# V of later batches loaded in single pieces at five places, and k's transposes over DRAM scratch issued a score step sooner, in a fused attention and SwiGLU kernel

## The chip, the cores and the metric

The kernel runs on one core of a Trainium2 chip. The metric is the device time of one execution in microseconds (us). The time before is the median of three runs.

## What is computed

Attention over 8 batches of 8 heads, 576 tokens and 64 channels, with a causal mask and a bias from a running sum; its output, as 4608 tokens of 512 channels, goes through a gated feed-forward block.

```python
scores = scale * np.matmul(q, k.transpose(0, 1, 3, 2))
cum = np.cumsum(np.maximum(s, 0.0), axis=-1)
bias = -(cum[:, :, :, None] - cum[:, :, None, :])
scores = np.where(causal, -1000000000.0, scores + np.minimum(bias, 0.0))
attn = softmax(scores)
attn_out = np.matmul(attn, v)
x = attn_out.transpose(0, 2, 1, 3).reshape(B * S, H * D)
out = (silu(x @ w_gate) * (x @ w_val)) @ w_out
```

## The kernel before

Each engine has its own queue and runs it in the order in which the program writes it; the program writes that order by hand. SP computes nothing: it issues DMAs, one after the other, and stops at one whose wait is not over.

**Attention.** The 64 heads are worked through in half-batches of 4 heads: half-batch `h`, score step `step` (0 to 3, one head), and in each step four pieces `ci` (0 to 3) of the score matrix. `score_piece` (line 352) lets PE multiply k and q (L373) into a PSUM bank and ACT write the exponentials to `pt` (L383). One step later PE multiplies `pt` with V (L410), and DVE divides by the row sums (L426, L427) into `ot`, which holds a pair of heads. There are 8 banks; a bank is free again when ACT or DVE has read it.

**The way of k and q.** Two half-batches ahead, SP loads k and q as float32 (`load_qk`, L145, tiles `rawk` and `rawq`), ACT casts them to bfloat16 (`cast_one`, L258, `ck` and `cq`), SP writes them to DRAM scratch (`scratch`, L274, `ks` and `qs`), SP reads them back transposed (`transposes`, L284, `pk` and `pq`, one buffer each), and DVE copies them to the operands of the score matmuls (`split`, L288). The splits wait in a list `later`, out of which `do_later` issues one for every two or four pieces of feed-forward work.

**The way of V.** Five pieces for each batch, 128 tokens of 8 heads in each (the last 64), loaded by SP (`load_v`, L162) into `rawv`, which has one buffer, and cast to `vt` by ACT (L171) in steps 1 to 3 of the batch's preceding odd half-batch. For batch 2 POOL casts (L173).

**The way of the output.** From batch 2 on, POOL stores each pair of heads to DRAM (`x_out`, L444, `xs`), and SP reads it back transposed (`x_in`, L451) into `XT`, two steps after the pair's last scores, in one or two parts. `XT` holds three token tiles of 512 tokens in a ring.

**Feed-forward.** There are nine token tiles `tt`. For each, PE multiplies XT with the weights of gate and value (L643), four contraction slices for each product, of which slice `c` is the pair of heads `c` of the batch; ACT takes a tanh (L664), DVE multiplies (`pp` L666, `ht` L677); then PE multiplies with the output weights (L700 for tiles 0 and 1, L749 for the rest). The main loop interleaves this with attention: after every piece of feed-forward work, attention goes on up to a set position. Tile 2 begins 3.6 steps after the scores of batch 2 are done.

**The places.** `side(h, step, ci)` is called behind every score piece and says what is issued there. For half-batches from 7 on: at step 0, piece 1 the raw loads of half-batch `h + 3`; at step 2, piece 0 both scratch writes of `h + 2`; at step 3, piece 0 the pending splits and both transposes of `h + 2`; in even half-batches V pieces 0 and 1 at step 2, piece 1 and pieces 2 to 4 at step 3, piece 1. For half-batch 6 (`six`, issued in `h = 4`) the places of scratch and transposes are step 3, piece 0 and step 3, piece 3. The XT transposes come behind the last piece of steps 1 and 3.

Of the kernel before, what the change touches and what calls it, by code (L numbers as in the profile page):

```python
# [19 lines left out]
def kernel(  # L20
# [11 lines left out]
    nc = tc.nc  # L32
# [10 lines left out]
    NR = HB // 2  # L43
    J = 9
# [37 lines left out]
    KS = {i: dram.tile([NR * S, 128], BF16, name=f"ks{i}") for i in range(NPE, NHB)}  # L82
# [3 lines left out]
    QS = {i: dram.tile([NR * S, 128], BF16, name=f"qs{i}") for i in range(NPE, NHB)}  # L86
# [27 lines left out]
    with tc.manual_schedule():  # L114
# [37 lines left out]
        def load_qk(hb):  # L152
            load_one(hb, "k")
            load_one(hb, "q")

        def load_v(b, cs, eng=nc.sync):
            if 0 in cs:
                loaded["v", b] = raw.tile([128, NCH, H, D], FP32, tag="rawv", bufs=1, name="rawv")
            t = loaded["v", b]
            for c in cs:  # L160
                n = 128 if c < 4 else TAIL
                eng.dma_start(  # L162
                    t[0:n, c, :, :],
                    v[b, :, c * 128 : c * 128 + n, :].rearrange("h p d -> p h d"),
                )

        def cast_v(b, c, eng):
            n = 128 if c < 4 else TAIL
            dst, src_t = VT[b % 2][0:n, c, :, 0:D], loaded["v", b][0:n, c, :, :]
            if eng is nc.scalar:  # L170
                nc.scalar.copy(dst, src_t)  # L171
            else:
                eng.tensor_copy(dst, src_t)  # L173
# [9 lines left out]
        def aug(hb, engs, hhs=range(HB)):  # L183
            for hh in hhs:
                r, e = divmod(hh, 2)
                r0 = 64 * (1 - r)
                bh = hb * HB + hh
                engs[hh].dma_start(  # L188
                    KQ[hb % 2][r][r0 : r0 + 4, :, e * S : (e + 1) * S],
                    HL[bh : bh + 1, :, :, :],  # L190
                )
# [61 lines left out]
        def cast_one(hb, name, eng):  # L253
            cts[name, hb] = cp.tile([128, J, NR, D], BF16, tag="c" + name, bufs=2, name="c" + name)
            dst = cts[name, hb].rearrange("x j r d -> x r j d")
            src_t = loaded[name, hb]
            if eng is nc.scalar:
                nc.scalar.copy(dst, src_t)  # L258
            else:
                eng.tensor_copy(dst, src_t)  # L260
# [8 lines left out]
            else:  # L269
                eng.tensor_copy(dst, src_t)  # L270

        def scratch(hb):
            for name, SC in (("k", KS), ("q", QS)):
                nc.sync.dma_start(  # L274
                    SC[hb].rearrange("(x j) c -> x (j c)", j=J),
                    cts[name, hb].rearrange("x j r d -> x (j r d)"),
                )

        prs = {}

        def transposes(hb):
            for name, SC in (("k", KS), ("q", QS)):
                prs[name, hb] = cp.tile([128, NR * S], BF16, tag="p" + name, bufs=1, name="p" + name)
                nc.sync.dma_start_transpose(prs[name, hb], SC[hb])  # L284

        def split(hb, name, r):
            kq = SRC[name][1]
# [181 lines left out]
        later = []  # L469

        def do_later(n):
            while n > 0 and later:
                f, *args = later.pop(0)
                f(*args)
                n -= 1
# [5 lines left out]
        def side(h, step, ci):  # L481
            bh = HB * h + step
            for c in V1_AT.get((bh, ci), ()):
                cast_v(1, c, nc.gpsimd)
            if bh == H + 4 and ci == 3:
                load_v(2, range(5))
            if h == 4 and (step, ci) in ((0, 1), (2, 1)):
                load_qk(6 + step // 2)
            if h >= 5 and h + 3 < NHB and (step, ci) == (0, 1):
                load_qk(h + 3)  # L490
            hb = h + 1
            if NPE <= hb < NHB:
                late = hb == NPE
                if late and (step, ci) == (0, 1):
                    scratch(hb)
                if late and (step, ci) == (0, 3):
                    transposes(hb)
                if (step, ci) == (0, 1):
                    aug(hb, GP4)
                first = 1 if hb < NPE + 3 else 0  # L500
                if step in (first, first + 1) and ci == (3 if late else 1):
                    for r in range(NR):
                        later.append((split, hb, "kq"[step - first], r))
            hb = h + 2
            if hb == NPE and step == 3 and ci % 2 == 1:
                cast_one(hb, "kq"[ci // 2], nc.gpsimd)
            if NPE < hb < NHB:
                six = hb == NPE + 1
                if (step, ci) == ((2, 0) if six else (0, 2)):
                    cast_one(hb, "k", nc.scalar)  # L510
                if (step, ci) == ((2, 2) if six else (1, 2)):
                    cast_one(hb, "q", nc.scalar)
                if (step, ci) == ((3, 0) if six else (2, 0)):
                    scratch(hb)
                if (step, ci) == (3, 3 if six else 0):
                    do_later(NR * 2)
                    transposes(hb)
            if ci != 1:
                return
            bn = h // 2 + 1  # L520
            if 3 <= bn < B:
                if h % 2 == 0:
                    if step == 2:
                        load_v(bn, (0, 1))
                    if step == 3:
                        load_v(bn, (2, 3, 4))

        V2_AT = {(1, 0): 0, (1, 1): 1, (1, 2): 2, (1, 3): 3, (2, 0): 4}
        V_AT = {(1, 0): 0, (2, 0): 1, (2, 2): 2, (3, 0): 3, (3, 2): 4}

        def side_v(h, step, ci):
            bn = h // 2 + 1
            if h == 4 and (step, ci) in V2_AT:
                cast_v(2, V2_AT[step, ci], nc.gpsimd)
            if 3 <= bn < B and h % 2 == 1 and (step, ci) in V_AT:
# [25 lines left out]
        def attn_items():  # L561
            for kk in range(H, BH + 2):
                h, step = divmod(kk, HB)
                if kk < BH:
                    if step == 0:
                        do_later(NR * 2)
                    if step == 1 and 3 < h + 1 < NPE:
                        cast_one(h + 1, "k", nc.gpsimd)
                        cast_one(h + 1, "q", nc.gpsimd)
                    if step == 2 and 3 < h + 1 < NPE:  # L570
                        aug(h + 1, GP4)
                    for ci in range(4):
                        score_piece(kk, ci)
                        side(h, step, ci)
                        side_v(h, step, ci)
                        yield kk + 0.1 + ci / 8
                        if (step, ci) in PREP_AT.get(h, ()):
                            prep_one(
                                h + 1, PREP_AT[h][step, ci],
                                (nc.scalar, nc.vector)[ci // 2] if h == 2 else None,  # L580
                            )
                            yield kk + 0.1 + ci / 8
# [327 lines left out]
        def pick(side):  # L910
            b = PICK[side]
            for lo in range(2):
                for c0, c1 in ((0, 512), (512, S)):
                    nc.tensor.matmul(
                        banks[:, b + c0 // 512, 0 : c1 - c0], sel[:, lo, :],
                        HL[:, lo, 1, c0:c1], start=(lo == 0), stop=(lo == 1),
                        skip_group_check=True,
                    )

        def picked_row(side):  # L920
            b = PICK[side]
            src_t = banks.rearrange("p b n -> p (b n)")[up, b * 512 : b * 512 + S]
            dst = KQ[0][0][up, side, 0:S]
            if side == 1:
                nc.scalar.activation(
                    dst, src_t, AF.Identity, bias=r_m[up, 0:1], scale=r_k[up, 0:1]
                )
            else:
                nc.vector.tensor_scalar(
                    dst, src_t, r_q[up, :], r_k[up, :], ALU.mult, ALU.add  # L930
                )
            give(b)
            give(b + 1)
# [102 lines left out]
        at = attn_items()  # L1036
# [84 lines left out]
```

## Time and profile before

| what | us |
|---|---|
| median of 3 runs | 374.26 (373.94 to 375.38) |
| the profiled execution | 373.92 |
| its span, first to last instruction | 372.0 |
| its granted TensorE clock | 0.998 of full speed |

The chain of work that ended last, by engine, and the two kinds of DMA queue (the hardware queue is SP's, the software queue POOL's):

```profile
PE 83%; DVE 10%; DMA 2%; ACT 2%; issue 2%; POOL 1%; DVEq 0%; ACTq 0%
...
q1 hardware_dynamic: 84964, 41.46, 46.9%
q0 software_dynamic: 12128, 22.21, 22.7%
```

The second and third line give packets, megabytes and the share of the 16 DMA engines' time. In a row of the order of time, the numbers are the start and the duration in us, then the engine (SPq: SP's queue), the line, what is written from what, how often, and in brackets the idle time before it and what ended it. For SP's DMAs the duration is that of the issue; when one has landed is seen in the semaphores, which count to sixteen for each DMA. In the waits, the three numbers are us in total, times, and the longest. A row of DMA packets counts those below a size cumulatively.

### The profile page before, as it was taken

How to read it: one execution, taken by the hardware profiler on the slowest of the kernel's cores; microseconds unless marked ns; L12 is line 12 of the kernel's file. 1: busy time of each engine (PE TensorE's matmuls, PEld its weight loads, DVE VectorE, ACT ScalarE, POOL GpSimd, SP SyncE). 2: the span in 40 equal slices, each digit the busy share in tenths (PEclk: the TensorE clock that was granted, in tenths of full speed). 3: DMA queues.
4: the chain of work that ended last, by engine and by line, in shares of the span. 5: the costliest groups of instructions: out<-in, count | busy, mean ns of one | idle time of the engine just before them, and what ended most of it. 6: DMA issues, size and time to landing. Idle time of an engine off the chain costs nothing.

```text
span 372.0 us, 8786 instructions
## 1 busy us (share of the span) xinstructions
PE 363.2 (98%) x3288; PEld 230.3 (62%) x3288; DVE 291.1 (78%) x585; ACT 239.9 (65%) x470; POOL 212.4 (57%) x325
## 2 busy tenths in 40 slices
PE   7899999999999999999999999999999999999996
PEld 6684556655555557855685558655865585476465
DVE  8978776377985899589967897699868867975984
ACT  8877776778886967688757875786565523323321
POOL 8983556955266547594749464955675516315320
PEclk9999999999999999999999999999999999999999
DMA  7999999799879996996789484994142113002003
GB/s 238 220 254 259 215 272 257 239 299 227 252 172 307 199 268 181 162 285 217 214 179 263 160 185 157 265 210 114 40 121 62 35 30 118 0 3 86 28 0 113
DMA packets 97133, 64.21 MB, mean 173 GB/s; under 512 B 77228, under 2 KB 82724, under 8 KB 97092
## 3 DMA queue, kind: packets, MB, share of 16 engines
q1 hardware_dynamic: 84964, 41.46, 46.9%
q0 software_dynamic: 12128, 22.21, 22.7%
q8 instruction: 25, 0.41, 0.5%
q14 instruction: 16, 0.13, 0.1%
HBM read 37.90 MB, written 19.86 MB: 155 GB/s over the span
## 4 chain that ended last, share of the span: by engine, by line
PE 83%; DVE 10%; DMA 2%; ACT 2%; issue 2%; POOL 1%; DVEq 0%; ACTq 0%
PE banks L643 43%; PE banks L749 17%; PE banks L373 9%; PE banks L410 7%; PE banks L700 5%; DVE kq L330 3%; DMA pk<-ks 2%; DVE pp L666 2%; DVE ht L677 1%; DVE kq L288 1%; ACT th L664 1%; POOL vt L173 1%; ACT pt L383 1%; PE banks L459 1%; PE banks L301 0%
## 5 line engine op out<-in xcount | busy, mean ns | idle before, releaser
L383 ACT ACTIVATE pt<-banks 128x512 bf16<-128x512 f32 (+1 forms) x256 | 120.4, 511 | 29.8 <-PE banks L373 17.1
L643 PE MATMUL banks<-XT,wg 128*128 128x512 bf16 x432 | 111.4, 379 | 0.4 <-DVE pp L666 0.3
L643 PE MATMUL banks<-XT,wv 128*128 128x512 bf16 x432 | 110.9, 379 | 0.1
L664 ACT ACTIVATE th<-banks 128x512 bf16<-128x512 f32 x108 | 64.7, 599 | 56.3 <-PE banks L643 51.4
L666 DVE SCALAR_TENSOR_TENSOR pp<-th,banks 128x512 bf16<-128x512 bf16 x108 | 73.7, 682 | 18.3 <-ACT th L664 18.0
L677 DVE SCALAR_TENSOR_TENSOR ht<-pp,banks 128x512 bf16<-128x512 bf16 x108 | 74.1, 687 | 10.3
L373 PE MATMUL banks<-kq 128*128 128x128 bf16 (+4 forms) x576 | 76.4, 240 | 0.8 <-DVE kq L330 0.3
L686 POOL TENSOR_TENSOR ht<-ht 128x512 bf16<-128x512 bf16 x35 | 40.4, 1154 | 53.3 <-DVE su L684 53.2
L373 PEld LDWEIGHTS <-kq 128*128 128x128 bf16 x576 | 46.1, 98 | 30.7 <-issue 2.4
L643 PEld LDWEIGHTS <-wv 128*128 128x128 bf16 x432 | 38.4, 98 | 36.2 <-issue 0.2
L643 PEld LDWEIGHTS <-wg 128*128 128x128 bf16 x432 | 38.4, 98 | 34.1 <-issue 0.7
L410 PEld LDWEIGHTS <-pt 128*128 128x128 bf16 x960 | 41.8, 98 | 17.7 <-issue 0.7
L388 POOL TENSOR_SCALAR_AFFINE_SELECT pt<-pt 128x512 bf16<-128x512 bf16 x56 | 36.6, 653 | 25.9 <-ACT pt L383 21.7
L410 PE MATMUL banks<-vt,pt 128*128 128x65 bf16 x960 | 46.8, 194 | 0.5 <-DVE ot L427 0.4
L444 POOL DMA_DIRECT2D xs<-ot x24 | 21.7, 904 | 30.4 <-DVE ot L427 28.0
L749 PEld LDWEIGHTS <-ht 128*128 128x128 bf16 x336 | 31.2, 98 | 4.3
L427 DVE TENSOR_TENSOR ot<-banks,rc 128x320 bf16<-128x320 f32 x64 | 31.5, 492 | 2.2
L188 POOL DMA_DIRECT2D kq<-HL x48 | 29.2, 610 | 0.0
L700 PE MATMUL banks<-wo,ht 128*128 128x512 bf16 x96 | 25.8, 379 | 0.0
L749 PEld LDWEIGHTS <-su 128*128 128x128 bf16 x252 | 23.6, 98 | 3.3
L814 POOL TENSOR_TENSOR ysb<-ysb 128x512 f32<-128x512 f32 x12 | 15.2, 1269 | 15.3 <-DVE ysb L808 15.3
L749 PE MATMUL banks<-WS,ht 128*128 128x256 bf16 x168 | 22.9, 273 | 0.0
(101 smaller groups left out, 377.2 us busy)
## 6 DMA issues: line engine op xcount, KB each, us to landing
out_dram<-ysb POOLq DMA_DIRECT2D x32, 256.0 KB, 4.0
rawv<-in_v_dram SPq DMA_DIRECT2D x28, 256.0 KB
rawk<-in_k_dram SPq DMA_DIRECT2D x12, 576.0 KB
rawq<-in_q_dram SPq DMA_DIRECT2D x12, 576.0 KB
xs<-ot POOLq DMA_DIRECT2D x24, 160.0 KB, 3.7
ks<-ck SPq DMA_DIRECT2D x11, 288.0 KB
qs<-cq SPq DMA_DIRECT2D x11, 288.0 KB
rawk<-in_k_dram POOLq DMA_DIRECT2D x3, 576.0 KB, 6.0
```

Source lines behind the costliest of these rows:

```text
L373: nc.tensor.matmul(sc[:, o : o + w], T[:, 1, e * S + 128 * tj : e * S + 128 * (tj + 1)], T[:, 0, e * S + lo : e * S + hi], start=not maske ...
L383: nc.scalar.activation(pt[:, c0 : c0 + n], sc, AF.Exp, scale=0.125)
L388: nc.gpsimd.affine_select(pt[:, 1088:1600], pt[:, 1088:1600], pattern=[[0, 4], [1, 128]], compare_op=ALU.is_ge, fill=zreg, base=0, channel ...
L410: nc.tensor.matmul(av[:, bi * (D + 1) : (bi + 1) * (D + 1)], pt[:, c0 : c0 + 128], VT[b % 2][:, tj, h, :], start=(tj == 0), stop=(tj == bi),)
L427: nc.vector.tensor_mul(ot[:, :, e * D : (e + 1) * D], av3[:, :, 0:D], rc[:, :, None].to_broadcast([128, NCH, D]),)
L643: nc.tensor.matmul(view(bs, TT), w[:, c, f0 : f0 + 128], xt[:, c, :], start=(c == 0), stop=(c == 3),)
L664: nc.scalar.activation(th, pg, AF.Tanh, scale=0.5)
L666: nc.vector.scalar_tensor_tensor(pp, in0=th, scalar=1.0, in1=pg, op0=ALU.add, op1=ALU.mult)
L677: nc.vector.scalar_tensor_tensor(hp[:, 2 * k2 : 2 * k2 + 2, :].rearrange("p a n -> p (a n)"), in0=pp, scalar=0.5, in1=pv, op0=ALU.mult, op ...
L686: (nc.vector if ft == NFT - 1 else nc.gpsimd).tensor_sub(hp[:, 1:3, :], hp[:, 1:4:2, :], hp[:, 0:3:2, :])
L700: nc.tensor.matmul(view(pys[ts_], DM), hps[ft // 2][:, 2 * (ft % 2) + half, c0 : c0 + 128], WO[j][:, ft % WKO, :], start=(ft == 0), stop=( ...
L749: nc.tensor.matmul(ps, lhs(p), rhs(p), start=(first and p == 0), stop=(last and p == NP - 1), skip_group_check=True,)
```

## The change

V from batch 3 on is no longer issued in groups of two and three pieces but one piece at each of five places: from batch 4 on at step 0 piece 3, step 1 pieces 0 and 2, step 2 piece 1 and step 3 piece 1 of the even half-batch; for batch 3, pieces 0 and 1 at step 2 pieces 1 and 3 of half-batch 4, and pieces 2 to 4 at step 0 pieces 1 and 3 and step 1 piece 1 of half-batch 5. The scratch write of k goes to step 1 piece 1 (q's stays), the transposes of k to step 2 piece 2 (q's stays at step 3 piece 0); for half-batch 6 to step 2 piece 1 and step 3 piece 1 (q's stay). Before the transposes of a name, only the pending splits up to the last of that name are issued.

```diff
-        def scratch(hb):
-            for name, SC in (("k", KS), ("q", QS)):
+        SCR = {"k": KS, "q": QS}
+
+        def scratch(hb, names="kq"):
+            for name in names:
                 nc.sync.dma_start(
-                    SC[hb].rearrange("(x j) c -> x (j c)", j=J),
+                    SCR[name][hb].rearrange("(x j) c -> x (j c)", j=J),
                     cts[name, hb].rearrange("x j r d -> x (j r d)"),
                 )
...
-        def transposes(hb):
-            for name, SC in (("k", KS), ("q", QS)):
+        def transposes(hb, names="kq"):
+            for name in names:
+                while any(args[1] == name for _, *args in later):
+                    do_later(1)
                 prs[name, hb] = cp.tile([128, NR * S], BF16, tag="p" + name, bufs=1, name="p" + name)
-                nc.sync.dma_start_transpose(prs[name, hb], SC[hb])
+                nc.sync.dma_start_transpose(prs[name, hb], SCR[name][hb])
...
+                if (step, ci) == ((2, 1) if six else (1, 1)):
+                    scratch(hb, "k")
                 if (step, ci) == ((3, 0) if six else (2, 0)):
-                    scratch(hb)
-                if (step, ci) == (3, 3 if six else 0):
-                    do_later(NR * 2)
-                    transposes(hb)
-            if ci != 1:
-                return
+                    scratch(hb, "q")
+                if (step, ci) == ((3, 1) if six else (2, 2)):
+                    transposes(hb, "k")
+                if (step, ci) == ((3, 3) if six else (3, 0)):
+                    transposes(hb, "q")
             bn = h // 2 + 1
             if 3 <= bn < B:
-                if h % 2 == 0:
-                    if step == 2:
-                        load_v(bn, (0, 1))
-                    if step == 3:
-                        load_v(bn, (2, 3, 4))
-
+                at = VLOAD_AT if bn > 3 else V3LOAD_AT
+                if (h % 2, step, ci) in at:
+                    load_v(bn, (at[h % 2, step, ci],))
+
+        VLOAD_AT = {(0, 0, 3): 0, (0, 1, 0): 1, (0, 1, 2): 2, (0, 2, 1): 3, (0, 3, 1): 4}
+        V3LOAD_AT = {(0, 2, 1): 0, (0, 2, 3): 1, (1, 0, 1): 2, (1, 0, 3): 3, (1, 1, 1): 4}
```

In a key of the two tables the first number is `h % 2`, the second the step, the third the piece; the value is the piece of V.

## Prediction

> **What bounds the kernel now.** I read the engine shares and the slices of the page first, then the waits (all, and SP's own), then PE, ACT and SP in order of time from 70 to 140 us, then the DMA packets of short stretches.
>
> ```profile
> span 372.0 us, 8786 instructions
> PE 363.2 (98%) x3288; PEld 230.3 (62%) x3288; DVE 291.1 (78%) x585; ACT 239.9 (65%) x470; POOL 212.4 (57%) x325
> ...
> DMA  7999999799879996996789484994142113002003
> ```
>
> PE sets the end. Its rows run at one pace (four 512-column matmuls take 0.86 us wherever the chain shows them after 35 us) at a granted clock of 0.998, so PE can only lose time by standing idle. It is idle 372.0 - 363.2 = 8.8 us. I listed the gaps: all but two (and a few below 0.1 us) lie before 35 us, which the change doesn't touch. These are the two, and what DVE waited for:
>
> ```profile
> 83.34 0.38 PE L373 MATMUL banks<-kq 128*128 128x128 bf16 x4 [0.26 <-DVE kq L288]
> 131.44 0.47 PE L410 MATMUL banks<-vt,pt 128*128 128x65 bf16 x10 [0.40 <-DVE ot L427]
> ...
> DVE kq L288 <- DMA pk<-ks: 1.7, 2, 1.0
> ```
>
> So nothing that the change can do for PE is worth more than 0.26 + 0.40 = 0.66 us, 0.18% of 374.26. What it can cost is open, since the DMA slices mostly read 6 to 9 until about 205 us: whatever SP issues sooner pushes back what it issues later. The place where that matters is the start of token tile 2, at 116.41 us:
>
> ```profile
> 107.81 0.57 SPq L145 DMA_DIRECT2D rawk<-in_k_dram  x1
> 108.44 0.46 SPq L145 DMA_DIRECT2D rawq<-in_q_dram  x1
> 108.94 2.45 SPq L451 DMA_TRANSPOSE XT<-xs  x2
> 111.50 0.53 SPq L274 DMA_DIRECT2D ks<-ck  x1
> 112.12 0.38 SPq L274 DMA_DIRECT2D qs<-cq  x1
> 112.55 1.81 SPq L162 DMA_DIRECT2D rawv<-in_v_dram  x2
> 118.37 2.59 SPq L284 DMA_TRANSPOSE pk<-ks  x1
> ...
> 116.41 1.02 PE L643 MATMUL banks<-XT,wg 128*128 128x512 bf16 x4
> ```
>
> The transpose at 108.94 brings heads 22 and 23 of batch 2 into XT. They are the last of the four contraction slices of tile 2, so the fourth matmul of that row needs them, at 116.41 + 3 x 0.215 = 117.05 us. In the trace's semaphore record the first of the two transposes (the part that tile 2 reads) gets its sixteenth completion at 116.31, 7.4 us after its issue. The margin is 0.74 us. The same difference for tiles 3 to 6 is 5.0, 5.4, 4.1 and 4.7 us.
>
> **The change part by part.** PE's, ACT's and POOL's instructions stay the same and in the same order; no bank is taken or given elsewhere. What moves is SP's queue, and in DVE's queue at most a split copy by a place or two.
>
> *Splits forced early.* The k transposes now first issue the pending k splits. They run (L288) at 92.67 and 94.97, 106.99 and 108.81, 125.62 and 129.93, each at or before the new place (step 2, piece 2, for instance 94.97 and 130.18). So nothing or one copy moves: 0.45 us on DVE at most, hidden behind DVE's other waits; 0 on PE.
>
> *K scratch and transposes sooner.* For half-batch 6 the k scratch moves from 80.48 to just behind its cast (the ACT cast at 74.36 takes 1.15, so 75.5), ahead of V pieces. Its transposes should land about 88 instead of 92.6, and those of half-batch 8 one or two us before 125.6. That ends DVE's two waits of 1.7 us together. Gain on PE: between 0 and 0.66; I take 0.40, the gap at 131.44, since it follows the wait at 125.62. The gap at 83.34 belongs to half-batch 5, which isn't moved.
>
> *V of batch 3, pieces 2 to 4 later.* They move from behind the q scratch of half-batch 6 (83.85) to behind the raw loads of half-batch 8. Before, SP issues those at 93.91, 4.1 us after the q transposes (89.80). The q transposes now wait only for q's scratch (issued about 80.5, landing about 87), so the raw loads start near 91.1 and, with the 5.7 us that they took to land (93.91 to 99.58 in the semaphore record), end near 96.8. A V piece more: near 98.2. Its cast wants it at 95.45:
>
> ```profile
> 95.45 0.64 ACT L171 CAST vt<-rawv 128x512 bf16<-128x512 f32 x1
> ...
> 97.34 0.62 ACT L171 CAST vt<-rawv 128x512 bf16<-128x512 f32 x1
> ...
> 99.67 0.61 ACT L171 CAST vt<-rawv 64x512 bf16<-64x512 f32 x1
> ```
>
> ACT waits some 2.7 us (0.5 if SP gets there 2 us sooner, 4 if q's scratch lands at 88.25 as before). Behind that cast stand exponentials and tanh (95.95, 96.37, 96.87), and DVE's `pp` waits for the tanh. PE goes on while PSUM banks are free. From 95.25 to 98.44 PE begins five banks in 3.2 us and, every fourth us or so, one for V; about 1.8 a us. A bank is held some 1.6 us (tanh 0.60, `pp` 0.68 and the wait between), so 3 of 8 are held, and 5 last 2.8 us, about as long as ACT's wait. PE loses little here, 0.3 us (0 to 2, as DVE is busy 6.6 of 7 us from 94 to 101 and can't catch up). If PE is late here it is late at 117 too, so this is inside the next term, not on top of it.
>
> *V of batch 4, three pieces ahead of XT.* This decides. Before, between the raw loads of half-batch 9 (107.81, 108.44) and the XT transposes (108.94) SP issues nothing. After the change stand there, in SP's program order, V pieces 0 and 1, the k scratch of half-batch 8, and V piece 2. What does one cost? A V piece is 128 x 8 = 1024 rows of 256 B, a scratch 128 rows of 2304 B. Two stretches with a full queue:
>
> ```profile
> DMA packets 2277, 1.25 MB, mean 313 GB/s; under 512 B 2065, under 2 KB 2065, under 8 KB 2277
> ...
> DMA packets 2925, 0.80 MB, mean 201 GB/s; under 512 B 2879, under 2 KB 2879, under 8 KB 2924
> ```
>
> The first is 80 to 84 us (beside stores of POOL), the second 86 to 90. So 1024 short rows take 4 x 1024 / 2065 = 1.98 us or 4 x 1024 / 2879 = 1.42 us. In 76 to 80 us the same view has 455 packets above 2 KB and 241 below 512 B: (4 - 241 x 1.4/1000) / 455 = 8 ns each, so a scratch is 1.0 us. Three pieces and one scratch: 5.3 us (1.42) to 6.9 us (1.98). I take 5.3, as the semaphore record has V pieces 1.3 to 1.4 us apart just after (120.44, 121.74).
>
> *SP sooner.* Against this, the raw loads of half-batch 9 may be issued sooner. They follow the XT transposes of the pair before, whose store lands at 103.38; with 2.5 us for those two, 105.9 is the earliest, 1.9 us before 107.81. In between lies SP's longest wait for a scratch, which the change means to hide:
>
> ```profile
> SPq L284 <- DMA ks<-ck: 20.7, 7, 4.0
> ```
>
> It ends at 102.6. But q's scratch of half-batch 7 is now issued behind V pieces and XT transposes, and its transposes stand ahead of the XT ones, so part of the wait is only handed from k to q. Between 0 and 1.9 I take 1.2.
>
> The sum: 116.31 + 5.3 - 1.2 = 120.4 for the landing, against 117.05: PE idle 3.4 us. Less the 0.40 above: +3.0 us. All later XT parts have 4 to 5 us of margin, gain 3 more from PE's delay, and are moved less, since SP waits there for the store (up to 9.2 us) and the V pieces are through by then: 0. The profiled run took 373.92 (span 372.0, 1.92 around it), 0.34 below the median of 374.26; added to the median, 377.3.
>
> The Trainium skill's page "DMA: Bandwidth & Descriptors" (section "Queues, rings and completion order") says that each DMA engine takes a queue's descriptors in ring order; this trace agrees (the sixteenth completions of SP's transfers from 107.81 to 118.37 come in the order of issue). The same page's fit for one DMA (section "Anatomy of one DMA"), 2.0 us + bytes / 436e3, speaks against my price, though it is given for GpSimd's path: with the fixed part overlapped, a 256 KB piece would move in 0.60 us, three in 1.8, and with the scratch at 0.68 XT would land at 117.6, which makes the kernel 0.1 us slower, an estimate. The rows decide, and they have a piece at 1.42.
>
> **The rivals.**
> *A, absorbed.* The pieces cost less than in the rows or SP is the full 1.9 us sooner: with pieces at 1.0 us (two of the batch 3 ones land 1.03 apart, 89.05 and 90.08), 116.31 + 4.0 - 1.9 = 118.4, so 1.3 idle, less 0.4: 375.2. For it: pieces do land 1.0 apart at times. Against: POOL's stores of tile 1 share the engines just then.
> *B, not slower.* The transposes land in time, because SP's 4.0 us wait at 98.6 falls away and the DMA engines' idle time at 101 to 104 (share 0.21) is filled, so that everything issued up to XT is done sooner. It decides if XT's part lands by 117.05. Price: the 0.40 to 0.66 of the gaps: 373.6 to 373.9. Against: the store at 103.38 holds SP whatever is in front, so at most 1.9 of 5.3 can come back.
> *C, both waits in full.* The V casts hold ACT for 4 us with pieces 3 and 4 late too, SP is not sooner, and the pieces cost 1.98: XT at 116.31 + 6.9 = 123.2, 6.2 idle, less 0.4: 380.0. The q scratch waiting behind V speaks for it; the short rows at 1.42 against.
> *D, no effect.* The new places could coincide with when SP gets there anyway; SP runs behind its program in 80 to 125 us, so order is all that counts, and the order does change. I see little for this apart from A and B.
>
> **How the numbers follow.** A measurement of this kernel tells about 0.5%, 1.9 us, from no change. Forecast (+1.9 to +5): 0.62. C: 0.08. A and what else stays within 1.9 us: 0.20. B: 0.10, of which 0.03 beyond 0.5%, from a gain that I don't see. Faster 0.03, same 0.27, slower 0.70. The forecast's own range is 376.2 to 379.2; the one for 8 in 10 takes in A and the better part of B: 373.9 to 379.3.
>
> **What would show it.** Right: a new PE gap of 2 to 5 us at the fourth matmul of tile 2 (about 117), ended by the XT transposes; ACT waiting for rawv near 95 to 98; DVE no longer waiting for pk; SP rows with rawv ahead of XT. After 125 us both kernels run in parallel, shifted by a constant. Wrong: XT landing before 117 with the V pieces ahead of it (then the price of a piece was off), the gap ended by ACT or DVE instead (then the casts decide), or PE losing time at tiles 3 to 6 (then the stores, slowed by V, are what is late).

## The result

| | before | after |
|---|---|---|
| median of 22 runs, us | 374.04 (373.23 to 378.62) | 379.38 (375.51 to 381.75) |
| ratio of the times | | 1.0111, 95% interval 1.0091 to 1.0130 |
| span of the profiled execution, us | 372.0 | 378.0 |

The change makes the kernel slower by 1.1%, some 4.2 us; the medians are 5.3 us apart and the two profiled executions 6.0. A ratio here is of fast executions alone, without those more than 1.5% above the quickest of the same kernel, while a median is of all. The page of the changed kernel (its lines stand four to five further down in the code):

```profile
span 378.0 us, 8753 instructions
PE 363.5 (96%) x3248; PEld 231.5 (61%) x3288; DVE 291.6 (77%) x585; ACT 240.0 (64%) x470; POOL 212.4 (56%) x325
...
PE 82%; DVE 8%; DMA 4%; ACT 2%; issue 2%; POOL 1%; SPq 1%; DVEq 0%; ACTq 0%
```

PE is as busy as before, 363.5 us against 363.2, and the span is longer: most of the time went into idle PE. (Forty matmul records are missing here, 3248 of 3288; each leaves a false gap of 52 or 53 ns, some 2.1 us together.) In the chain the DMAs' share is 4% where it was 2%. These are PE's rows around the two places, with the idle time and what ended it in brackets:

```profile
99.58 0.19 PE L377 MATMUL banks<-kq 128*128 128x64 bf16 x1 [0.79 <-ACT pt L387]
100.79 1.02 PE L648 MATMUL banks<-XT,wv 128*128 128x512 bf16 x4 [1.02 <-DVE pp L671]
...
118.51 0.81 PE L648 MATMUL banks<-XT,wg 128*128 128x512 bf16 x3
121.92 0.38 PE L648 MATMUL banks<-XT,wg 128*128 128x512 bf16 x1 [2.60 <-DMA XT<-xs]
...
122.63 1.67 PE L648 MATMUL banks<-XT,wv 128*128 128x512 bf16 x4
124.09 1.91 PE L648 MATMUL banks<-XT,wg 128*128 128x512 bf16 x4
```

The first two gaps begin with ACT. Its cast of V piece 2 of batch 3, which stood at 95.45 before, waits:

```profile
98.79 0.62 ACT L171 CAST vt<-rawv 128x512 bf16<-128x512 f32 x1 [3.24 <-DMA rawv<-in_v_dram]
```

The third is the fourth matmul of token tile 2: XT isn't there. And behind it four matmuls take 1.67 and 1.91 us in place of 1.03, though PE waits for nothing. The windows of 2 us show why (busy us and instructions of PE, PE's weight loads, DVE, ACT and POOL; then the granted clock, the DMA share and GB/s):

```profile
120.00:122.00 2.00, 0.08 (x1) 0.08 (x1) 0.00 (x0) 0.00 (x0) 0.44 (x1) 1.00 0.69 161
122.00:124.00 2.00, 2.00 (x18) 1.02 (x18) 0.94 (x3) 1.08 (x2) 0.45 (x1) 0.72 0.99 376
124.00:126.00 2.00, 2.00 (x6) 0.76 (x5) 1.49 (x3) 0.00 (x0) 2.00 (x5) 0.50 1.26 264
```

The granted clock is 0.50 from 122.87 to 126.28 us. SP's rows (the number is the start and the duration of the issue) show how XT came to be late:

```profile
109.35 0.57 SPq L145 DMA_DIRECT2D rawk<-in_k_dram  x1
109.97 0.49 SPq L145 DMA_DIRECT2D rawq<-in_q_dram  x1
110.56 1.16 SPq L162 DMA_DIRECT2D rawv<-in_v_dram  x2
111.81 3.52 SPq L276 DMA_DIRECT2D ks<-ck  x1
115.38 0.43 SPq L162 DMA_DIRECT2D rawv<-in_v_dram  x1
115.91 3.57 SPq L455 DMA_TRANSPOSE XT<-xs  x2
```

Between the raw loads and the XT transposes stand three V pieces and a scratch, and XT is issued at 115.91 instead of 108.94. By the semaphore record its part for tile 2 lands at 121.88 instead of 116.31. SP wasn't waiting for the store of that pair of heads: POOL's store landed at 111.34, 4.6 us before XT was issued.

The same exponential of both kernels, found by its number on ACT, says where the 6.0 us arise:

| exponential, before at | after at | later by | what lies between |
|---|---|---|---|
| 92.97 | 92.97 | 0.0 | |
| 101.6 | 103.7 | 2.1 | V cast, 0.79 + 1.02 of PE's idle time |
| 118.0 | 122.9 | 4.9 | XT at tile 2 |
| 123.5 | 130.0 | 6.55 | clock at half rate, 1.7 |
| 133.2 | 139.2 | 6.0 | the gap at 131 is gone, which gives 0.56 |
| 293.45 (last) | 299.44 | 6.0 | nothing in the last 160 us of attention |

### The profile page after: what moved, and what is told of

Read it like the earlier page. It is cut to its first block, busy times and chain, and to the rows that moved or that the text cites. A ratio compares the mean times of both kernels' runs of the same rounds, so it can differ in the third digit from the quotient of the medians.

```text
span 378.0 us, 8753 instructions
## 1 busy us (share of the span) xinstructions
PE 363.5 (96%) x3248; PEld 231.5 (61%) x3288; DVE 291.6 (77%) x585; ACT 240.0 (64%) x470; POOL 212.4 (56%) x325
## 4 chain that ended last, share of the span: by engine, by line
PE 82%; DVE 8%; DMA 4%; ACT 2%; issue 2%; POOL 1%; SPq 1%; DVEq 0%; ACTq 0%
PE banks L648 43%; PE banks L754 17%; PE banks L377 9%; PE banks L414 7%; PE banks L705 4%; DVE kq L334 2%; DMA rawv<-in_v_dram 2%; DMA XT<-xs 2%; DVE pp L671 2%; DVE ht L682 1%; DMA kq<-HL 1%; ACT pt L387 1%; POOL vt L173 1%; ACT th L669 1%; PE banks L463 1%
## 5 line engine op out<-in xcount | busy, mean ns | idle before, releaser
L705 PE MATMUL banks<-wo,ht 128*128 128x512 bf16 x90 | 24.8, 379 | 0.3
L397 POOL TENSOR_SCALAR_AFFINE_SELECT pt<-pt 128x64 bf16<-128x64 bf16 x56 | 14.9, 266 | 17.4 <-ACT pt L387 17.2
```

Of the source, the lines that this page charges most:

```text
L705: nc.tensor.matmul(view(pys[ts_], DM), hps[ft // 2][:, 2 * (ft % 2) + half, c0 : c0 + 128], WO[j][:, ft % WKO, :], start=(ft == 0), stop=( ...
```

## The experiments

The theory: V of batch 3 behind the raw loads stops ACT, and V of batch 4 ahead of XT stops PE. The rivals: the new order of k's scratch and transposes costs the time; a late store decides; single pieces cost as such. Times are medians; ratios are to the kernel before on the same chip. Executions of one kernel differ by some us, often because of the first 60 us, where no version differs. So the profiles are compared by one stretch: from the exponential at 63.51 us to the last one, which takes 229.94 us in the kernel before. Landings in this table, and times of SP that are compared between versions, are given less what the execution had lost by the exponential at 63.51. The stretch and the landing are of one execution of each version.

| version | median us | ratio (95%) | stretch against before | XT lands |
|---|---|---|---|---|
| before | 374.0 to 375.1 | 1 | 0 | 116.3 |
| the change | 379.4 | 1.0111 (1.0091 to 1.0130) | +6.0 | 121.9 |
| k's moves alone | 375.0 | 1.0017 (0.9988 to 1.0046) | +1.0 | 115.9 |
| V alone | 379.5 | 1.0111 (1.0057 to 1.0166) | +1.7 | 119.3 |
| V of batch 4 back | 375.6 | 1.0049 (1.0017 to 1.0081) | +1.7 | 119.3 |
| V of batch 3 back | 378.8 | 1.0063 (1.0023 to 1.0102) | +4.6 | 120.6 |
| the same again | 377.5 | 1.0039 (1.0004 to 1.0074) | +1.4 | 119.0 |
| the same, PE kept busy | 378.0 | 1.0103 (1.0058 to 1.0148) | +2.6 | 120.2 |
| V of batches 3 and 4 back | 375.5 | 1.0007 (0.9972 to 1.0041) | -0.6 | 116.7 |
| one piece behind XT | 378.1 | 1.0072 (1.0038 to 1.0107) | +1.8 | 119.3 |
| the change, PE kept busy | 379.4 | 1.0098 (1.0061 to 1.0134) | +7.0 | 123.5 |
| all V behind XT | 374.8 | 0.9994 (0.9961 to 1.0026) | -0.6 | 115.6 |

**One half of the change at a time.** First k's scratch and transposes alone:

```diff
                 at = VLOAD_AT if bn > 3 else V3LOAD_AT
-                if (h % 2, step, ci) in at:
+                if True:
+                    if (h % 2, ci) == (0, 1) and step in (2, 3):
+                        load_v(bn, (0, 1) if step == 2 else (2, 3, 4))
+                elif (h % 2, step, ci) in at:
                     load_v(bn, (at[h % 2, step, ci],))
```

> Only the k scratch and the k transposes are moved; V stays in its groups of two and three. Theory (the V pieces cost the time): one scratch of about 1 us stands ahead of the XT transposes of heads 22 and 23, against 0.74 us of margin and a sooner SP, so PE waits 0 to 0.3 us at tile 2, ACT never waits for rawv, DVE's waits for pk go: 373.3 to 374.3 us, ratio 0.998 to 1.001. Rival (the new order of scratch and transposes costs the time): PE waits 2 us or more at tile 2, 377 us or more.

No difference is measured (at most 0.46%, by the interval), and the rival that blames this order falls. Not as expected: DVE's waits for `pk` don't go, they grow from 1.7 to 2.7 us, since the k transposes still stand behind V pieces 0 and 1.

V alone, with both scratch writes and both transposes at their old places:

```diff
-                if (step, ci) == ((2, 1) if six else (1, 1)):
-                    scratch(hb, "k")
                 if (step, ci) == ((3, 0) if six else (2, 0)):
-                    scratch(hb, "q")
-                if (step, ci) == ((3, 1) if six else (2, 2)):
-                    transposes(hb, "k")
-                if (step, ci) == ((3, 3) if six else (3, 0)):
-                    transposes(hb, "q")
+                    scratch(hb)
+                if (step, ci) == (3, 3 if six else 0):
+                    do_later(NR * 2)
+                    transposes(hb)
```

> Only V is loaded piece by piece; scratch and transposes stay together at their old places. Theory: ACT waits for rawv at about 95 us as in the changed kernel (3 us, 2 of them PE's); XT of heads 22 and 23 has three pieces of V ahead and no scratch, so PE waits 1 us less than 2.6 at tile 2, and the clock halves or not: ratio 1.008 to 1.014. Rival (the order of k and q costs): ratio below 1.003.

The loss is here, 1.0111 again (six runs). PE's wait at tile 2 is 1.56 us, 1.04 less than in the changed kernel:

```profile
119.35 0.38 PE L645 MATMUL banks<-XT,wg 128*128 128x512 bf16 x1 [1.56 <-DMA XT<-xs]
```

That the difference is the one expected for the scratch is in part an accident. XT lands 2.6 us sooner, but 1.8 of that come from q's raw load, which lands sooner (113.73 against 115.57); and PE comes to tile 2 1.5 us sooner, because V held ACT for only 1.7 us. Some 0.7 us are left for the scratch. This profiled execution was one of the quick ones (375.64), with the clock at 1.00 behind both waits.

**Batch 3 or batch 4.** The edit is that of the first experiment, with `bn == 4` or `bn == 3` in place of `True`.

> The changed kernel with the V pieces of batch 4 alone at the old places and in the old groups. Theory: ACT still waits 3.2 us for V of batch 3 and PE loses 2.1 us at 98 to 101; the XT transposes of heads 22 and 23 land at 117 to 118 us, before PE asks at 119; no wait there, no clock drop, and the gap of 0.56 us at 131 stays away: 1.5 us over before, 375.6, ratio 1.004. Rival (the wait at tile 2 comes from a late store or from the scratch, not from V pieces ahead): PE still waits 2 us or more for XT, ratio as the changed kernel's, 1.011.

The time is the expected one, 375.6. Its profile is not quite: ACT waits 2.30 us for V and PE loses 1.02 there, but PE then also waits 0.89 us for XT, with no V piece ahead of it. XT is issued at 110.6 and lands 8.7 us later, behind a k scratch that is equally slow (its sixteenth completion comes 0.5 us ahead of XT's). So not every late XT is due to V ahead of it. The packet record shows what happened just before: from 120.6 to 122.3 us fifteen packets of POOL's stores took up to 1.70 us each and ended together, and almost nothing else moved (the last number is GB/s):

```profile
121.00:122.00 1.00, 0.93 (x10) 0.41 (x9) 1.00 (x2) 0.72 (x3) 1.00 (x3) 1.00 0.06 6
```

The scratch's sixteenth completion comes at the end of this standstill of the DMA engines, XT's half a microsecond later. The changed kernel has one too, from 119.4 to 121.4:

```profile
120.00:121.00 1.00, 0.00 (x0) 0.00 (x0) 0.00 (x0) 0.00 (x0) 0.44 (x1) 1.00 0.51 49
```

In each of the eight profiles in which PE waits for XT at tile 2 or is kept busy there, such a standstill, with packets of 1.2 to 2.0 us, ends 0.4 to 1.1 us ahead of XT's landing. But so it does (113.6 to 115.2) in the last version below, where XT is in time. What causes it, and how much later XT comes by it, no run here shows.

> The changed kernel with the V pieces of batch 3 alone at the old places. ACT doesn't wait for rawv in either theory. Theory (the two waits of PE overlap: XT lands when SP's queue lets it, whatever PE lost before): XT of heads 22 and 23 still lands near 121 us, PE comes 2.1 us sooner and waits 4 to 4.7 us at tile 2, the clock halves: ratio 1.010 to 1.015, nothing gained. Rival (the two waits add): PE waits 2.6 us and the time falls by 2.1 us, ratio 1.005.

PE's row at the fourth matmul of tile 2:

```profile
121.16 0.38 PE L651 MATMUL banks<-XT,wg 128*128 128x512 bf16 x1 [3.38 <-DMA XT<-xs]
```

ACT doesn't wait, PE reaches tile 2 sooner and waits longer, 3.38 us, and the clock halves, from 122.27 to 125.69. But the ratio lies below the theory's 1.010 and near the rival's 1.005, and an identical kernel, run later beside the version below, gave this:

> The kernel with V of batch 3 at the old places again, beside its version with matmuls in the wait, on the same chip. Both theories: PE waits 3 to 4 us for XT at tile 2 and the granted clock is 0.50 for some 3.5 us behind it; ratio to before 1.006 to 1.015.

Its wait was 1.83 us, the clock stayed at 1.00, and the ratio was 1.0039. So the waits don't simply overlap: with V of batch 3 out of the way, SP itself is sooner. The raw loads of half-batch 9 go out at 107.5 and 106.0, against 109.4 in the changed kernel and 108.9 with V of batch 3 alone late. On the time the two batches roughly add up: 0.5% for batch 3, 0.4 to 0.6% for batch 4, each within 0.3 to 0.4 either way, and 1.1% together. Even an identical kernel has XT land 1.5 us apart in two executions (120.6 and 119.0).

**Neither.** With `bn <= 4` in the same edit:

> The changed kernel with V of batches 3 and 4 at the old places and in the old groups; the five single places only from batch 5 on, and k's scratch and transposes moved. Theory (all the loss lies in batches 3 and 4): ACT doesn't wait for rawv, PE waits at most 0.3 us at tile 2, tiles 3 to 6 start without a wait: 373.5 to 374.5 us, ratio 0.998 to 1.002. Rival (the single places cost at tiles 3 to 6 as well, by stores that are slowed): PE gaps of 0.5 us or more there, ratio over 1.003.

No difference to the kernel before, no PE gap above 0.35 us behind 20 us: the five places cost nothing that shows at tiles 3 to 6.

**One piece.**

```diff
+        V4LOAD_AT = {(0, 0, 3): 0, (0, 1, 0): 1, (0, 2, 0): 2, (0, 2, 1): 3, (0, 3, 1): 4}
...
-                at = VLOAD_AT if bn > 3 else V3LOAD_AT
+                at = VLOAD_AT if bn > 4 else V4LOAD_AT if bn == 4 else V3LOAD_AT
```

> The changed kernel with V piece 2 of batch 4 alone moved behind the XT transposes of heads 22 and 23; all five pieces stay single. Theory (each piece ahead of XT costs what it takes to move): XT lands 1.3 us sooner, PE waits 1.0 to 1.6 us instead of 2.6 at tile 2, and with the shorter gap the granted clock stays at 1.00 behind it: 376 to 377.5 us, ratio 1.006 to 1.009. Rival (a late store decides): the wait stays at 2 us or more, ratio 1.010 or more.

The ratio is the expected one; the wait isn't, 2.18 us:

```profile
121.69 0.38 PE L649 MATMUL banks<-XT,wg 128*128 128x512 bf16 x1 [2.18 <-DMA XT<-xs]
```

In this execution V of batch 3 held ACT for only 0.23 us, so PE came 2 us sooner than in the changed kernel's profile. XT's landing tells more: 119.3 against 121.9, 2.5 us sooner. But 1.7 of these come from raw loads issued sooner, which the edit doesn't touch; 0.9 are left for the piece. The late store is not what decides: it lands at 111.09, 5 us before XT is issued at 116.19. The clock stayed at 1.00 behind this gap.

**The clock.** PE gets something to do in the wait, here in the changed kernel with 44 matmuls, then with V of batch 3 back and 54:

```diff
-                gbs = products("g", ft, xt)
+                if (tt, ft) == (2, 0):
+                    gbs = take()
+                    block("g", 0, xt, gbs, range(3))
+                    spare = take()
+                    keep_warm(44, spare)
+                    give(spare)
+                    block("g", 0, xt, gbs, range(3, 4))
+                else:
+                    gbs = products("g", ft, xt)
```

> The changed kernel with 44 matmuls of 128 columns on the identity, 2.5 us of work that nobody reads, between the third and the fourth matmul of tile 2, where PE waits. Theory (the idle time itself makes the clock halve afterwards): the gap before the fourth matmul is 0 to 0.7 us, the granted clock stays 1.00 from 122 to 127, PE begins the second gate product 1.7 us sooner: 1 to 1.7 us faster than the changed kernel, ratio 1.006 to 1.008. Rival (the clock drops there for another reason): it still halves, and the ratio is 1.011 or more.

At tile 2 there is no gap and no drop. But in this execution V of batch 3 held ACT for 4.59 us, PE was idle for 2.15 and 1.02 us with 0.19 of work between, and the clock halved there, from 103.08 to 106.49. So it didn't separate the two, and the time is not the expected one: 1.0098, as for the changed kernel itself.

> The kernel with V of batch 3 at the old places (no wait of ACT for rawv, PE idle 3.4 us at tile 2, clock halved from 122.3) with 54 matmuls of 128 columns that nobody reads, 3.0 us of work, between the third and fourth matmul of tile 2. Theory (idle time makes the clock halve): gap at most 0.6 us, clock 1.00 from 118 to 128, the stretch behind it 1.7 us shorter; 1 to 1.7 us faster than the same kernel without them. Rival (the clock halves there whether PE works or not): clock 0.50 behind the fourth matmul, no difference in time.

Two windows of this version, where the kernel without the added matmuls had 0.57 and 0.58 from 122 to 126 in its first profile:

```profile
122.00:124.00 2.00, 2.00 (x13) 1.01 (x12) 1.97 (x6) 1.12 (x3) 2.00 (x4) 1.00 1.30 285
124.00:126.00 2.00, 2.00 (x25) 1.17 (x24) 1.65 (x4) 2.00 (x4) 1.14 (x3) 1.00 1.25 87
```

The clock stays up, although XT landed 2.97 us after the end of the third matmul (117.24 to 120.21), longer than the 2.60 us of idle time behind which it halved in the changed kernel. It is one execution; the expected gain of 1 to 1.7 us didn't come: 1.0103 against 1.0039 beside it, with intervals that meet. Where XT comes sooner, the added matmuls take time themselves (54 of them took 3.18 us).

**Other places.** Single pieces, but all behind the XT transposes of step 1, and batch 3 in its even half-batch:

```diff
-        VLOAD_AT = {(0, 0, 3): 0, (0, 1, 0): 1, (0, 1, 2): 2, (0, 2, 1): 3, (0, 3, 1): 4}
-        V3LOAD_AT = {(0, 2, 1): 0, (0, 2, 3): 1, (1, 0, 1): 2, (1, 0, 3): 3, (1, 1, 1): 4}
+        VLOAD_AT = {(0, 2, 0): 0, (0, 2, 1): 1, (0, 2, 3): 2, (0, 3, 1): 3, (0, 3, 3): 4}
+        V3LOAD_AT = {(0, 2, 1): 0, (0, 2, 3): 1, (0, 3, 0): 2, (0, 3, 1): 3, (0, 3, 2): 4}
```

> Single V pieces and the moved k scratch and transposes as in the change, but the places of V lie behind the XT transposes of step 1: from batch 4 on step 2 pieces 0, 1, 3 and step 3 pieces 1, 3; for batch 3 step 2 pieces 1, 3 and step 3 pieces 0, 1, 2 of the even half-batch. Theory: nothing but one scratch stands ahead of XT at tile 2 and V of batch 3 lands before its cast: no wait of ACT for rawv, PE gap at tile 2 at most 0.3 us, 373.3 to 374.5 us, ratio 0.997 to 1.002. Rival (single pieces cost as such): ratio over 1.004.

SP's rows of this version ahead of XT:

```profile
106.32 0.57 SPq L145 DMA_DIRECT2D rawk<-in_k_dram  x1
106.94 0.46 SPq L145 DMA_DIRECT2D rawq<-in_q_dram  x1
107.50 0.41 SPq L276 DMA_DIRECT2D ks<-ck  x1
111.20 2.42 SPq L455 DMA_TRANSPOSE XT<-xs  x2
```

And PE's row of the same version at the start of tile 2:

```profile
116.49 1.02 PE L648 MATMUL banks<-XT,wg 128*128 128x512 bf16 x4
```

The scratch that takes 3.52 us to issue behind two V pieces takes 0.41 here, and SP then waits for POOL's store, which lands at 111.19. PE has its four matmuls in one row, and the gap at 131 us is gone: the stretch is 0.6 us shorter than before. In the time it is no different from the kernel before (0.9994, 0.9961 to 1.0026), and clearly faster than the change.

## Why the prediction was right, and where its sizes were off

The forecast was 377.3 us, slower by 3.0, with a PE wait for XT at the fourth matmul of tile 2 as the place. The direction, the place and what ends the wait came out so; the size is short: 1.1% or 4.2 us, which on the median of the forecast (374.26) is 378.4 and inside its range; the median of 379.38 lies just above both ranges, 376.2 to 379.2 and 373.9 to 379.3. By its steps:

- **What can be won.** The gap at 131 us went, as forecast for 0.40; it gave 0.56 us. DVE no longer waits for `pk`.
- **Splits.** As forecast: DVE and PE show nothing of them.
- **V of batch 3.** ACT's wait was put at 2.7 us and was 3.24 in the changed kernel's profile, and 0.23 to 4.59 in others. PE's part of it was mis-sized: 0.3 forecast, 1.8 measured here, and 0 to 3.2 in the other profiles. Five free banks didn't last, since DVE stood still for the tanh as well (3.13 us) and gave none back. And it was taken to be inside the wait at tile 2; the runs show that it also makes SP late, by 1.8 to 3.4 us at the raw loads of half-batch 9 (107.5 and 106.0 without it, 109.35 with it), and that on the time it adds some 0.5%.
- **Three pieces and a scratch ahead of XT.** Put at 5.3 us. From the landing of q's raw load to XT's it is 6.3 us after (115.57 to 121.88) and 1.2 before (115.08 to 116.31): 5.1. The sum is right, but by parts that make up for each other. Each of the pieces lands 1.19, 1.18 and 0.87 us behind what is ahead of it, where 1.42 was forecast; the scratch lands 2.70 us behind, where 1.0 was. SP is held at that scratch's issue for 3.52 us, and the standstill from 119.4 to 121.4 falls into the same stretch; the sum had neither.
- **SP sooner by 1.2.** This is the term that had the wrong sign: the raw loads went out 1.5 us later (109.35 for 107.81) and landed 0.5 later. In the versions with V of batch 3 in its old place they are indeed 0.3 to 2.5 us sooner; the step left out that the change's own V pieces hold SP before.
- **The sum.** XT was to land at 120.4 and landed at 121.88. PE had lost 2.1 us before, so its idle time there is 2.60 us in place of the 3.4 forecast; the two losses add. On top came a cost that no row of the kernel before could show, the halved clock, 1.7 us in the profiled execution. Rival C's price of 380.0 is nearest to that execution (379.99), but of its three conditions only one holds: SP isn't sooner. ACT's wait was 3.24 us and not 4, and the pieces took 1.2 us or less and not 1.98.
- **Tiles 3 to 6.** No wait, as forecast.
- **The skill page's fit for one DMA**, as the prediction cites it, would have made the change 0.1 us slower. With V pieces 1.2 us apart in the record of the changed kernel (115.57, 116.76, 117.94 for q's raw load and the two pieces), the rows were the better guide.

Open: how often an execution of the changed kernel meets the halved clock at tile 2. The mean granted clock is 0.995 or less in 15 of its 22 runs and 0.998 or more in the other seven (medians 379.67 and 377.16), but other drops, in the first 20 us of some executions, make the same mean. In the kernel before, 12 of the 80 runs with a clock on record have 0.995 or less, and with V of both batches back 2 of 12. But with PE kept busy at tile 2 it is still 7 of 11, and the time isn't lower, so the drops of the change are not all at tile 2, and their 1.7 us are shown for the profiled execution, not for the median. What makes the DMA engines stand still ahead of XT is open as well.

## What to carry to other kernels

Before a load is moved forward in an in-order DMA queue, look for the transfer with the least time to spare that it now stands ahead of, and compare that margin (here 0.74 us) with the moved bytes' time in a full queue (5 us). A load that is early enough gains nothing by being earlier; its place is behind the transfers that are waited for. If PE is the bound and idles for more than some 2.2 us, look at the granted clock behind the gap too.

## What the runs showed of the hardware

- **The clock halves behind an idle PE.** From 60 us on it did after gaps of 2.60 and 3.38 us, and after 2.15 and 1.02 with 0.19 of work between; it didn't after 1.56, 1.83 and 2.18 alone. In the 3.41 us ahead of these three drops PE was idle for 2.47, 2.30 and 2.30 us; in the profiles without a drop there, no stretch of 3.41 us held more than 2.18. These are single executions, and in the first 20 us of two others the clock drops behind 1.7 us of idle time in such a stretch, so idle time isn't the whole rule. Each of the three drops stayed at 0.50 for 3.41 or 3.42 us; in the changed kernel's profile that cost 1.7 us. The Trainium skill's page "TensorE: Matmul & The Clock Gate" (section "What's actually happening") gives a free-running window of about 3.4 us for both directions; the length of the drops agrees. The same page's advice (section "Why this matters for your kernels") to keep gaps below about 3 us is too wide for this case: 2.60 us was enough.
- **A DMA issue can hold SP for 3 us.** In the changed kernel six scratch writes took 2.90 to 3.86 us to issue, each right behind two V pieces of up to 1024 rows; the other sixteen took 0.35 to 0.57. The kernel before has one such, 2.85 us at 80.48, behind two V pieces too. With V alone moved it is the third V piece that is held, 3.03 us. In five of the six SP goes on 0.14 to 0.25 us before the sixteenth completion of the transfer just ahead of the two V pieces (at 115.33, with q's raw load landing at 115.57), so the issue seems to wait for the queue to empty that far; what limits it no run here shows.
